# Fused attention and mixture of experts on one core: seven routing turns in each pair of heads instead of five

## The chip, the cores and the metric

The kernel runs on one core of a Trainium2 chip. The metric is the device time of one execution in microseconds (us). The engines of a core work side by side, each on its own queue in order: PE (TensorE, matmuls), DVE (VectorE), ACT (ScalarE), POOL (GpSimd) and SP (SyncE, which issues DMAs here). An instruction waits at the head of its engine's queue until what it reads is there and what it writes is free.

## The reference

Causal attention with a decay bias over 8 batches of 8 heads, 576 positions and 64 columns, and then a mixture of 16 experts in 4 groups, one expert for each of the 4608 tokens:

```python
scores = scale * np.matmul(q, k.transpose(0, 1, 3, 2))
cum = np.cumsum(np.maximum(s, 0.0), axis=-1)
bias = -(cum[:, :, :, None] - cum[:, :, None, :])
scores = np.where(causal, -1000000000.0, scores + np.minimum(bias, 0.0))
attn = np.exp(scores - np.max(scores, axis=-1, keepdims=True))
attn = attn / (np.sum(attn, axis=-1, keepdims=True) + 1e-09)
x = np.matmul(attn, v)                  # turned to (4608, 512)
g_idx = np.argmax(x @ w_group, axis=1)  # one group for each token
e_idx = np.argmax(xg @ w_expert[g], axis=1)  # one expert in that group
ye = np.maximum(xg[mask_e] @ w1[g, e], 0.0) @ w2[g, e]
out[tok_idx] = combined[:, None] * ye   # weighted by both softmax values
```

## The kernel before

Attention works through 64 heads, one head in each step, two heads (a pair) in an even and an odd step. In a step PE runs three kinds of matmuls, taken in turn: A, the scores of a head four steps ahead for its row maxima (`pm`, line 220, six items A0 to A5); B, the transposed scores of this step's head for the exponentials (`ps`, lines 276 and 278); and C, the product of the probabilities of the head before with the values (`po`, line 316).

What the other engines do with these goes through small queues of Python closures: a letter in the order pops one. `a` is DVE's maximum (`mx`, line 228), which reads a `pm` buffer and so gives it back; there are two such buffers, and `keep("a", 1)` pops the older maximum before a third matmul is written. `b` is ACT's exponential, `e` POOL's causal mask, `v` ACT's copies of `po`, `T` and `t` the turned row maxima (`pmt`, then `th` and `tl`, lines 248 and 249), `Y`, `Z`, `W`, `K` the softmax division on DVE (line 344, 350, 355 and `xT`, line 363), `L` and `M` the split of `xT` (ACT, then POOL's `xTl`, line 380), `O` and `o` the turned rows of x, `S` and `G` the split of the next heads' inputs on ACT and POOL.

The order is written out by hand in two strings, one for even and one for odd steps. `R` in them is a turn of the router, `J` a turn only late in the kernel. `Router.batch` is a generator: each turn runs it to its next `yield`, and a `yield n` lets n turns pass unused. One batch of 8 heads (four pairs) gives 576 tokens to route, in this order: the logits (`lg`), the tail's logits and its rows (`pr`), the logits turned (`plt`, three copies on DVE), the group maxima (lines 813 to 821, `lmx`, `eq`, `fx`), the choice as ones (`oh`, `hot`), the counts (`pc`, then `off` and `pos`), the places (`us`, `pl`), `col`, `rows`, two products on POOL, the first listing (`pi`) with `df`, the weights (`w` to `cw`, lines 909 to 916), their parts (`c3`, POOL), three products (`val`, one on POOL and two on DVE), and the last listing (`pw`). From the first turn to the last that makes 26 turns with the unused ones.

A pair has five turns, four pairs 20. What is left of a batch runs in one go, without the unused turns, when the next but one is about to write its `xT`: `rt.read` in `high` loops

```python
        while self.queue and self.logged < b - 1:
            self.step(True)
```

and so ends one batch and starts the next. In the order of the instructions this stands once in each batch, in an odd step, from the third batch's heads on. DVE, ACT, POOL and PE all follow the written order in this stretch; in the last steps of attention (from step 62) only PE does, and a scheduler orders the other engines.

After attention the experts run one after the other: tokens gathered by index, two matmuls, rows scattered to the output.

Of the kernel before, what the change touches and what calls it, by code (L numbers as in the profile page):

```python
# [19 lines left out]
B, H, S, D = 8, 8, 576, 64  # L20
# [33 lines left out]
def attn_moe(ctx, tc, qk, v, s, wr, w1, w2, out, stop_at=None, dbg=None):  # L54
# [23 lines left out]
    st.listed, st.added = {}, {}  # L78

    attention(tc, qk, v, s, wr, xs, st)  # L80
    if dbg is not None:
        nc.sync.dma_start(dbg['x'], xs)
# [32 lines left out]
def attention(tc, qk, v, s, wr, xs, st):  # L115
# [3 lines left out]
    with ExitStack() as ctx:  # L119
# [405 lines left out]
        for t in VT:  # L525
# [8 lines left out]

        ORDERS = [o.split() for i, o in enumerate((
            "b S R B0 R v b a A0 B2 v C0 e G a R a B3 T C1 A3 B1 A2 C2 b e t C3 v G C4 B4 J b D v e a a A1 "
            "W e A4 C5 e C6 b a A5",
            "C0 B2 A4 B0 A2 S v e O C1 B1 B3 v X o A0 a Y L b J A3 a v a e b C2 b R K e M C3 G e b Q "
            "e C4 v A1 Z B4 a R A5 C5 b C6 t a a"))]
        FIRST = [o.split() for i, o in enumerate((  # L540
            "B4 b e A1 a R B0 b e B1 b C0 A0 a R J T t C1 v v D A2 a R W C2 B2 b e O o Q A3 a R B3 b e e A4 a "
# [6 lines left out]
        for step in range(-LEAD, NH + 5):  # L548
            m, a = step + LEAD, step - 1
# [1159 lines left out]
```

## Time and profile before

| | us |
|---|---|
| runs of the kernel | 876.05, 881.72, 1372.2 |
| their median | 881.72 |
| the profiled execution | 876.57 |
| its span, first to last instruction | 874.8 |
| PE busy in the span | 840.2 (96%) |
| DVE busy | 718.9 (82%) |
| ACT busy | 615.7 (70%) |
| POOL busy | 603.2 (69%) |

The span is 1.8 us shorter than the profiled execution's time. Busy time of PE is made of matmuls whose ends are modelled; where a wait matters, the starts of neighbouring matmuls say more than the idle figure behind a row. A row of the timeline gives the start and the time in us, the engine, the line, the operation, the tiles written and read, and in brackets the idle time before it and what ended it.

### The profile page before, as it was taken

The numbers are of one execution on the slowest core, as the hardware profiler recorded it, in microseconds if no ns is written. First come the engines' busy times: TensorE is split into PE (matmuls) and PEld (weight loads), VectorE is DVE, ScalarE is ACT, GpSimd is POOL, SyncE is SP. The second block draws the span as 40 slices with busy tenths as digits, with TensorE's granted clock in tenths as the row PEclk, the third lists the DMA queues.
The fourth block names the chain that finished last, engine by engine and source line by source line (L and its number), as shares of the span: only waits on it lengthen the run. The fifth ranks groups of instructions, "written<-read, shape, count | busy, mean of one in ns | idle before, by whom it ended". The sixth has DMA issues, their size and how long they took to land. (4 is left out here: it accounts for less than half of the span.)

```text
span 874.8 us, 17801 instructions
## 1 busy us (share of the span) xinstructions
PE 840.2 (96%) x5601; PEld 774.2 (89%) x5601; DVE 718.9 (82%) x1975; ACT 615.7 (70%) x1397; POOL 603.2 (69%) x746
## 2 busy tenths in 40 slices
PE   4999999999999999998799999999999999999997
PEld 2788888888888888886689999999999999999996
DVE  7567787787878788787468799999999999999972
ACT  5668777787868777776656656776677767777760
POOL 9767677676877768545657956776777777777660
PEclk9999999999999999999899999999999999999999
DMA  6999898897979898723546655555656565666620
GB/s 189 256 246 253 233 243 225 218 244 195 251 208 241 224 238 209 180 63 121 173 137 216 219 175 202 203 175 187 228 202 195 182 220 198 235 211 223 218 94 26
DMA packets 81877, 174.06 MB, mean 199 GB/s; under 512 B 9676, under 2 KB 45132, under 8 KB 73584
## 3 DMA queue, kind: packets, MB, share of 16 engines
q1 hardware_dynamic: 71664, 152.93, 59.6%
q0 software_dynamic: 7488, 18.89, 5.8%
q10 hardware_dynamic: 2624, 1.03, 0.5%
q8 instruction: 46, 0.75, 0.3%
q14 instruction: 55, 0.45, 0.2%
HBM read 108.97 MB, written 19.69 MB: 147 GB/s over the span
## 5 line engine op out<-in xcount | busy, mean ns | idle before, releaser
L1016 POOL TENSOR_TENSOR wl<-raw,wh 128x512 fp32r<-128x512 f32 x163 | 209.7, 1299 | 82.4 <-ACT wh L1013 58.6
L1013 ACT CAST wh<-raw 128x512 fp32r<-128x512 f32 x256 | 153.9, 616 | 1.8 <-issue 1.8
L228 DVE CUSTOM_DVE_ANT_0 mx<-pm,mask 128x192 bf16<-128x192 f32 (+4 forms) x320 | 127.2, 418 | 31.4 <-PE pm L220 28.7
L1133 PE MATMUL ph<-xh,wh 128*128 128x256 f32 (+13 forms) x512 | 140.3, 300 | 1.8 <-DVE hl L1140 1.8
L220 PE MATMUL pm<-WA 66*128 66x288 f32 (+4 forms) x384 | 123.8, 355 | 15.3 <-DMA WA<-ch 9.5
L276 PE MATMUL ps<-WA 68*128 68x320 f32 (+4 forms) x384 | 135.9, 358 | 2.0 <-DMA WA<-tl 1.9
L1133 PE MATMUL ph<-xl,wh 128*128 128x256 f32 (+13 forms) x512 | 137.8, 301 | 0.0
L316 PE MATMUL po<-pt,VT 128*128 128x256 f32 (+3 forms) x512 | 119.4, 352 | 1.3 <-issue 1.0
L1212 PE MATMUL py<-hh,wh 128*128 128x256 f32 (+13 forms) x448 | 112.9, 302 | 0.0
L1212 PE MATMUL py<-hl,wh 128*128 128x256 f32 (+13 forms) x448 | 112.4, 301 | 0.0
L1139 ACT ACTIVATE hh<-ph 128x256 fp32r<-128x256 f32 (+13 forms) x128 | 53.3, 418 | 83.8 <-PE ph L1133 82.9
L278 PE MATMUL ps<-WB 128*128 128x320 f32 (+4 forms) x384 | 110.7, 301 | 0.0
L1265 DVE STREAM_TRANSPOSE yr<-yT 32x384 f32<-32x384 f32 (+1 forms) x208 | 104.6, 503 | 4.5 <-ACT yT L1209 0.4
L316 PE MATMUL po<-pu,VT 128*128 128x320 f32 (+1 forms) x384 | 105.5, 383 | 1.3 <-POOL pu L295 1.3
L1103 DVE STREAM_TRANSPOSE xt<-xg 32x256 f32<-32x256 f32 (+1 forms) x208 | 102.4, 492 | 2.7
L316 PEld LDWEIGHTS po<-pt,VT 128*128 128x128 f32 x512 | 88.2, 192 | 13.9 <-issue 1.5
L1133 PEld LDWEIGHTS ph<-xh,wh 128*128 128x128 f32 x512 | 95.9, 190 | 2.1 <-DVE hl L1140 1.9
L1133 PEld LDWEIGHTS ph<-xl,wh 128*128 128x128 f32 x512 | 95.2, 190 | 0.2
L162 POOL TENSOR_TENSOR WB<-r,hl 64x576 fp32r<-64x576 f32 x62 | 88.0, 1420 | 6.1 <-DMA WB<-hl 1.8
L1133 PE MATMUL ph<-xh,wl 128*128 128x256 f32 (+13 forms) x512 | 92.0, 299 | 0.0
L220 PEld LDWEIGHTS pm<-WA 66*128 66x128 f32 (+1 forms) x384 | 69.2, 193 | 25.1 <-DVE mc L228 9.8
L380 POOL TENSOR_TENSOR xTl<-xT,xTh 128x512 fp32r<-128x512 f32 x30 | 38.2, 1272 | 76.0 <-ACT xTh L376 55.4
(249 smaller groups left out, 2007.3 us busy)
## 6 DMA issues: line engine op xcount, KB each, us to landing
raw<-in_w_dram SPq DMA_DIRECT2D x64, 1024.0 KB
r<-in_qk_dram SPq DMA_DIRECT2D x32, 576.0 KB
WA<-hl SPq DMA_DIRECT2D x60, 288.0 KB
WB<-hl SPq DMA_DIRECT2D x60, 288.0 KB
VT<-in_v_dram SPq DMA_DIRECT2D x32, 384.0 KB
WB<-hl SPq DMA_DIRECT2D x64, 144.0 KB
xs<-xr SPq DMA_DIRECT2D x15, 512.0 KB
WA<-cumd SPq DMA_DIRECT2D x56, 4.5 KB
```

Of the source, the lines that this page charges most:

```text
L162: (nc.vector if p < 1 else nc.gpsimd).tensor_tensor(out=hl[:, 2] if part else WB[p % NBB][0:64, KA, h], in0=r[hr, part], in1=hl[hr, part]. ...
L220: nc.tensor.matmul(ps[:rows, :cw], WA[i][0:66, QA, h, QO + q0:QO + q0 + rows], WA[i][0:66, KA, h, QO + c0:QO + c0 + cw], start=True, stop= ...
L228: nc.vector.tensor_tensor_reduce(out=tmp[:rows, :cw], in0=ps[:rows, :cw], in1=mk[:rows], scale=1.0, scalar=-3.0e38 if c0 == 0 else mo, op0 ...
L276: nc.tensor.matmul(ps[:rows, o:o + w], WA[i][0:68, KA, h, QO + k0:QO + k0 + rows], WA[i][0:68, QA, h, QO + q0:QO + q0 + w], start=True, st ...
L278: nc.tensor.matmul(ps[:rows, o:o + w], WB[p % NBB][:, KA, h, k0:k0 + rows], WB[p % NBB][:, QA, h, q0:q0 + w], start=False, stop=True)
L316: nc.tensor.matmul(po[0][:, qa - base:qb - base], VT[p % NVT].rearrange("p t a d -> p (t a d)")[:, (3 * t + 1 + h) * 64:][:, 0:P], x[:, c: ...
L1013: self.casts.append(nc.scalar.copy(h[:, j], raw[:, j]))
L1016: self.low = lows[self.u, i, j] = nc.gpsimd.tensor_tensor(out=l[:, j], in0=raw[:, j], in1=h[:, j].bitcast(F32), op=ALU.subtract)
L1103: V.transpose(dst[:, 0:n, :, j], src[:, 0:n, :, i])
L1133: self.product = nc.tensor.matmul(pss[f][:, :cap], w[f // 4][:, c, (f % 4) * P:(f % 4 + 1) * P], x[:, c, :cap], start=(c == 0 and w is sel ...
L1212: self.product = nc.tensor.matmul(pss[c][:, :cap], w[2 + f // 4][:, f % 4, c * P:(c + 1) * P], x[:, f, :cap], start=(f == 0 and w is self. ...
L1265: V.transpose(dst[:, 0:n, :, i], src[:, 0:n, :, j])
```

## The change

Each of the two strings gets one more `R`: in the even step behind A4, in the odd step behind the first `S`.

```diff
         ORDERS = [o.split() for i, o in enumerate((
             "b S R B0 R v b a A0 B2 v C0 e G a R a B3 T C1 A3 B1 A2 C2 b e t C3 v G C4 B4 J b D v e a a A1 "
-            "W e A4 C5 e C6 b a A5",
-            "C0 B2 A4 B0 A2 S v e O C1 B1 B3 v X o A0 a Y L b J A3 a v a e b C2 b R K e M C3 G e b Q "
+            "W e A4 R C5 e C6 b a A5",
+            "C0 B2 A4 B0 A2 S R v e O C1 B1 B3 v X o A0 a Y L b J A3 a v a e b C2 b R K e M C3 G e b Q "
             "e C4 v A1 Z B4 a R A5 C5 b C6 t a a"))]
```

A pair then has seven turns and a batch's four pairs 28. Which turn of a batch falls where changes for all of them; from the last batch on every engine has the order of before. On each engine the set of instructions is the same.

On DVE, before, in the pair of steps in which `col` and `rows` run (`mx` is a maximum, `mc` its accumulator read back): `col` stands before the reciprocal of the odd step, `rows` before that step's last maximum.

```order
L228 ISA mx_2_0_3455,mc_155<-pm_2_0_3450,mask 128x320
L228 ISA mc_155 128x1
L868 TENSOR_TENSOR col_3462<-hot,u_3322 128x320
L350 RECIPROCAL rc_3473<-st_3446 128x18
L228 ISA mx_0_0_3478,mc_155<-pm_0_0_3471,mask_150 64x64
L228 ISA mc_155 64x1
L873 TENSOR_TENSOR rows_3480<-cols,pl_3341 128x640
L228 ISA mx_4_288_3487,mc_155<-pm_4_288_3482,mask,mc_155 128x288
```

The two places that `col` and `rows` leave hold other turns now.

On DVE, now, the same two turns: the first stands between the transpose of line 355 and the 64-wide maximum of the even step, the second between the last maximum of the even step and the 448-wide one of the odd step.

```order
L355 STREAM_TRANSPOSE st_3083<-rc_3111 128x576
L868 TENSOR_TENSOR col_3218<-hot,u_3152 128x320
L228 ISA mx_0_0_3223,mc_156<-pm_0_0_3213,mask_150 64x64
L228 ISA mc_156 64x1
L363 TENSOR_TENSOR xT_3231<-vals_2828,st_3083 128x576
L228 ISA mx_3_0_3240,mc_156<-pm_3_0_3216,mask 128x448
L228 ISA mc_156 128x1
L228 ISA mx_4_288_3247,mc_156<-pm_4_288_3225,mask,mc_156 128x288
L228 ISA mc_156 128x1
L873 TENSOR_TENSOR rows_3252<-cols,pl_3171 128x640
L228 ISA mx_3_0_3274,mc_156<-pm_3_0_3242,mask 128x448
```

Both now stand in places that held no turn before. In the other pairs of a batch the even place takes the copies of `plt`, the weights and the last lists, and the odd place the group maxima and the start of `c3`.

On PE, before, in the odd step in which one batch ends and the next begins: the last listing and the logits stand in one piece between two of the step's own matmuls.

```order
L886 MATMUL pw_3028<-val_2717,rows_2696 128x192
L733 MATMUL lg_3036<-xTh_2262,wr_sb 40x512
L734 MATMUL lg_3036<-xTl_2263,wr_sb 20x512
...
L737 MATMUL lg_3036<-xTh_2262,wr_sb 40x512
L220 MATMUL pm_4_0_3053<-WA_107 128x288
L220 MATMUL pm_2_0_3061<-WA_107 128x320
L316 MATMUL po_1_3069<-pt_118,VT_116 128x320
```

The burst is gone now, and its parts stand as turns of their own.

On PE, now, in an even step: the turned logits, which stood behind the burst, come right after the step's two neighbouring row-maximum matmuls.

```order
L278 MATMUL ps_4_0_2990<-WB_115 64x64
L220 MATMUL pm_0_0_3002<-WA_107 64x64
L220 MATMUL pm_3_0_3005<-WA_107 128x448
L801 MATMUL plt_3007<-ident,lT 128x128 x4
L316 MATMUL po_1_2978<-pu_121,VT_117 128x320 x2
L220 MATMUL pm_4_288_3021<-WA_107 128x288
```

The logits stand in the odd step there too, alone behind its 64-row items, the last listing has a turn of its own in an even step, and two turns lie between the two.

## Rows read from the trace of the kernel before

**Rows 1.** Windows, a plain pair and a batch's four: stretch, its length, busy times.

```profile
73.60:84.52 10.92, 10.92 (x72) 9.76 (x70) 7.98 (x30) 9.15 (x24) 8.13 (x13) 1.00 0.94 268
219.25:230.50 11.25, 11.25 (x79) 10.04 (x78) 9.60 (x39) 9.14 (x24) 7.71 (x13) 1.00 0.97 272
230.50:241.88 11.38, 11.38 (x77) 10.01 (x75) 10.60 (x36) 9.33 (x25) 10.69 (x15) 1.00 0.88 233
241.88:256.20 14.32, 14.12 (x94) 11.81 (x93) 10.58 (x39) 10.25 (x27) 9.18 (x18) 1.00 0.79 216
256.20:268.12 11.92, 11.73 (x76) 10.30 (x74) 10.10 (x39) 9.33 (x26) 7.91 (x13) 1.00 0.77 199
```

The busy times are those of PE, its weight loads, DVE, ACT and POOL, each with its instructions, then the granted clock, the DMA share and GB/s.

**Rows 2.** Timeline of PE in the burst between two batches.

```profile
201.42 0.59 PE L886 MATMUL pw<-val,rows 128*128 128x192 bf16 x5
...
203.69 0.45 PE L220 MATMUL pm<-WA 66*128 66x288 f32 x2
...
205.52 0.62 PE L787 MATMUL pr<-xtl,wr_f 128*20 128x64 f32 x8 [0.20 <-ACT xr L415]
...
206.27 0.38 PE L220 MATMUL pm<-WA 66*128 66x288 f32 x1
...
207.80 0.60 PE L801 MATMUL plt<-ident,lT 128*128 128x128 f32 x4
208.16 0.38 PE L220 MATMUL pm<-WA 66*128 66x288 f32 x1
```

**Rows 3.** Timeline of DVE in the plain pair.

```profile
78.07 0.08 DVE L228 DVE_READ_ACCUMULATOR2_ANT mc<- 64x1 f32 x1
...
79.83 0.08 DVE L228 DVE_READ_ACCUMULATOR2_ANT mc<- 128x1 f32 x1
80.39 0.62 DVE L228 CUSTOM_DVE_ANT_0 mx<-pm,mask 128x448 bf16<-128x448 f32 x1 [0.47 <-PE pm L220]
80.94 0.08 DVE L228 DVE_READ_ACCUMULATOR2_ANT mc<- 128x1 f32 x1
```

**Rows 4.** Timeline of PE in the plain pair, row-maximum matmuls.

```profile
76.34 0.25 PE L220 MATMUL pm<-WA 66*128 66x192 f32 x1
...
77.57 0.51 PE L220 MATMUL pm<-WA 66*64 66x64 f32 x2
...
78.75 0.53 PE L220 MATMUL pm<-WA 66*128 66x288 f32 x1
...
81.98 0.46 PE L220 MATMUL pm<-WA 66*128 66x288 f32 x2
```

**Rows 5.** Timeline of PE, the same two matmuls in the pair after the burst.

```profile
210.51 0.25 PE L220 MATMUL pm<-WA 66*128 66x192 f32 x1
...
212.06 0.75 PE L220 MATMUL pm<-WA 66*64 66x64 f32 x2 [0.15 <-DVE mc L228]
```

**Rows 6.** Timeline of DVE, a maximum's end and routing turns.

```profile
211.94 0.07 DVE L228 DVE_READ_ACCUMULATOR2_ANT mc<- 128x1 f32 x1
...
229.98 2.09 DVE L873 TENSOR_TENSOR rows<-cols,pl 128x640 bf16<-128x640 f32 x1
...
241.71 0.25 DVE L909 TENSOR_REDUCE w<-df 128x25 f32<-128x100 f32 x1
...
243.07 0.45 DVE L228 CUSTOM_DVE_ANT_0 mx<-pm,mask 128x288 bf16<-128x288 f32 x1
```

**Rows 7.** Timeline of POOL, in the plain pair and beside `rows`.

```profile
81.98 1.27 POOL L380 TENSOR_TENSOR xTl<-xT,xTh 128x512 fp32r<-128x512 f32 x1 [2.60 <-ACT xTh L376]
...
229.98 1.41 POOL L162 TENSOR_TENSOR hl<-r,hl 128x576 fp32r<-128x576 f32 x1
```

**Rows 8.** Instructions by tile, `eq` and `rows`: ns least, median, most.

```profile
L817 DVE TENSOR_TENSOR eq<-logit,lmx x8: 264/981/983, 109.4 to 433.7; 128x100 f32<-128x100 f32 x8
L873 DVE TENSOR_TENSOR rows<-cols,pl x8: 811/1578/2102, 122.2 to 442.3; 128x640 bf16<-128x640 f32 x8
```

**Rows 9.** Timeline of PE, the turned logits of the seventh batch.

```profile
400.57 0.66 PE L801 MATMUL plt<-ident,lT 128*128 128x128 f32 x4 [0.92 <-ACT lT L791]
```

## What the change should do to the time

> **What bounds the kernel now.** I read the windows by pair of heads first. TensorE (PE) fills its span in nearly every stretch: a pair of heads without routing takes 10.92 us and PE is busy for all of it, while VectorE (DVE) is busy for 7.98 us. The four pairs that carry one batch's routing take 11.25, 11.38, 14.32 and 11.92 us, 48.87 together, which is 5.19 us over four plain pairs [rows 1]. So a batch's routing costs 5.19 us in all, and nothing that the order does can give back more than the part of it in which PE waits.
>
> That part comes out of PE's timeline in the third and fourth pair, where the burst stands [rows 2]. The last listing matmuls and the next batch's logits run without a gap, 201.42 to 203.69, 2.27 us; the tail's logits and transposes take 0.75 us (205.52 to 206.27), the transposes back 0.36 us (207.80 to 208.16). With 0.33 us for the counts (the first pair's excess) and about 0.3 us for the first listing (an estimate: 5/8 of the work of the last, most of the second pair's 0.46 us), PE's own routing work is 4.0 us. What waits is 5.19 - 4.0 = 1.2 us a batch, some 7 us in the six batches that the change rearranges. That is 0.8% of the profiled execution: **the change cannot make the kernel 2% faster.**
>
> The Trainium skill (Perfetto Trace Analysis, Tensor Engine Instruction) says that a matmul's end in the trace is an estimate from its size. The trace agrees: the matmul at 212.06 shows 0.15 us idle before it, but it starts 1.55 us after its forerunner, against 1.23 us in a plain pair [rows 4, 5], so it waited 0.32 us. By the idle figures the waits of a batch would be about 0.4 us, 2 us in all; by the starts they are 7.
>
> **Where PE waits for DVE.** Each row-maximum matmul writes one of two pm buffers; DVE's maximum (mx) gives it back. The slack is read from a plain pair. After the 64-wide maximum DVE lets go at 78.15 (78.07 + 0.08) [rows 3], and the matmul that reuses that buffer starts at 78.75 [rows 4]: 0.60 us. The 448-wide maximum of the odd step lets go at 81.02, and its successor starts at 81.98: 0.96 us; before it DVE has 0.47 us idle (79.91 to 80.39). From a release to the matmul go 0.05 us, read where PE did wait: released at 212.01 (211.94 + 0.07) [rows 6], started at 212.06 [rows 5]. So lateness beyond 0.55 us at the 64-wide maximum, or beyond 0.47 + 0.9 at the 448-wide one, is paid by PE in full. At the other places of a pair DVE waits for PE and has more room; the five turns of before stand there.
>
> **The change part by part.** It adds a turn in the even step, on DVE between the transpose L355 and the 64-wide maximum, and one in the odd step, just before the 448-wide maximum. These are the two tightest places. No instruction is added or dropped; SP's and POOL's queues get the same DMAs and operations, a batch's rows of x go out a step or two sooner, and nobody reads them before the experts. A batch needs 26 turns and has 28 instead of 20, so no remainder is left to be run at once.
>
> *Removed:* the burst, with its waits: 7 us by the above. The tail's logits no longer stand behind a turned block that ACT has just to copy out, and the group maxima no longer stand ahead of th and tl. PE's 4.0 us a batch are only moved.
>
> *Added at the even place*, by the order of DVE:
> - plt: DVE, in order, waits there for PE's four transposes, which stand right after the two matmuls of the even step that follow each other. With the 0.36 us on PE and three small copies (0.4 us, an estimate at half of L817's best price each, [rows 8]) the 64-wide maximum comes some 0.8 us late against PE: 0.3 us of wait.
> - col: half as many elements as rows, so 0.4 us at its best price [rows 8], and DVE up to 0.3 us late already, since the turn before th stays there: 0.2 us.
> - the weights (L909 to L916), 241.71 to 243.07, 1.36 us [rows 6]: 1.36 - 0.55 = 0.8 us. Before, they lay where DVE had room.
> - the last lists: as plt, 0.2 us.
>
> *Added at the odd place:*
> - the group maxima (L813 to L821): their price hangs on L817, 0.26 us at best and 0.98 at the median [rows 8]. With three more of its size at 0.26 us each the turn takes 1.1 or 1.8 us.
> - rows: 0.81 us at best, 2.10 at worst [rows 8]. At 229.98 it starts together with a POOL operation of 1.41 us, and takes 2.09 [rows 6, 7]: it stands until POOL is through.
>
> Which end holds is read from POOL: at the odd place it is idle for 2.60 us until xTl at 81.98 [rows 7], so from 79.4 on, and the turn starts at about 79.9. I take the short ends, 1.1 and 0.81 us. Then the group maxima, with 0.55 us of lateness left from plt, come 0.55 + 1.1 - 0.47 = 1.2 us late against 0.9: 0.3 us, and 0.1 for the matmul behind. Rows: 0.5 + 0.8 - 0.5 = 0.8 against 0.9: 0.1 at most. For the later matmuls of these two odd steps, where DVE is still behind and 0.2 to 0.5 us of room is left, I add 0.3 us.
>
> Sum per batch: 0.3 + 0.2 + 0.8 + 0.2 + 0.4 + 0.1 + 0.3 = 2.3 us, six times: 13.8 us. Bounds: 1.0 (only the weights' wait is sure; a DVE that catches up sooner takes the rest) and 5 (below, both odd turns and the weights at their long price).
>
> The Trainium skill (SBUF — State Buffer, Who interferes with whom) states that a DVE instruction with two SBUF inputs and a GpSimd instruction that reads SBUF exclude each other for the whole instruction, whoever comes first. The two prices of rows fit that. By this rule the odd place, where POOL rests, has the short price, and my sum stands; if the long price belongs to the operation itself, the second rival holds.
>
> *The end of attention:* batch 6 is taken through sooner, with other work between its tail logits and its transposes, where PE now waits 0.92 us [rows 9]; I count 1.5 us less with the shorter waits around it, between 0 and 2.5. The last batch stands where it stood, and from there on the order is the same on every engine; PE is what the next stage waits for, so a shift arrives in full.
>
> Sum: 13.8 - 7 - 1.5 = **+5.3 us** on the profiled execution's 876.57 us: 881.9. The runs of before shown are 876.05 and 881.72 us (the third, 1372.2, is left aside) and the profiled one is at their low end; I put the median at 2 us over that sum: **884 us**, against 881.72 within measurement.
>
> **The rivals.**
> - *The burst's end pays.* DVE is in time at the new places (PE's own routing work, moved, gives it room), and PE waits 0.5 us a batch: 3 - 7 - 1.5 = -5.5 us, 871 us profiled, 873 as a median. For it: DVE is idle a quarter of a plain pair. Against it: that idle time does not lie at the new places.
> - *POOL is not idle there* (slower). The lock decides: if POOL's splits slide into the odd place (they follow ACT and DVE, which come later too), rows cost 2.1 us and the group maxima 1.8, and the weights' two products each stand behind a POOL operation at the even place. Per batch the waits are then about 1.5 (plt and maxima), 1.7 (col and rows), 1.7 (weights) and 0.2: 5.1 us, six times 31; 31 - 7 - 1.5 = +22 us, 899 profiled, 900 as a median. It passes 2% (17.5 us) from 4.3 us of wait a batch. For it: L817's median is the long price. Against it: the 2.60 us of POOL's idle time.
> - *The turns change nothing that PE feels*: waits as large as before, 876 to 879 us. That the turns stay empty is ruled out: the order moves the listings of every batch from the first to the sixth by several turns.
>
> **How the numbers follow.** My forecast 0.58, with 879 to 891; the burst's end 0.20; POOL not idle 0.12, of it two thirds past 2%; nothing felt 0.10. The range takes in the first rival's 873 and reaches into the second, to 896. Faster by over 2%, 0.01; within 2%, 0.91; slower by over 2%, 0.08. Two per cent is about what a measurement of this kernel can tell from no change.
>
> **What would show it.** Windows by pair over a batch: the pair of 14.32 us gone, the excess spread over all pairs, and in sum about 6.3 us a batch (4.0 + 2.3) in place of 5.19. PE's pm waits for DVE behind the weights (about 0.8 us by starts) and behind the group maxima. L817 at 0.3 and rows at 0.8 us. If they stay at 0.98 and 2.1, the second rival holds; if the sum over a batch is under 4.6, the first. The prediction is wrong if PE waits for ACT or POOL instead, which I count at nothing because both have idle time in every pair (ACT 9.15 and POOL 8.13 us busy of 10.92, [rows 1]).

## The result, and the profile after

The changed kernel takes 889.61 us (median of four runs, 884.56 to 892.48), the kernel before 880.04 us beside it (median of four; one of them, 1372.2 us, was disturbed and is left out of the ratio, and the median of the other three is 878.35). The ratio is **1.0135, 95% interval 1.0105 to 1.0164**: slower, by less than 2%. The profiled execution took 884.56 us, its span is 882.8 us; before it was 876.57 and 874.8.

Attention explains it. A step is counted from item B0 of its head, the 256 columns of transposed scores. From step 11 to step 60 the kernel before takes 297.32 us and the changed one 310.68: +13.4. From step 60 on they are alike to 0.8 us. Up to the start of step 5 it took 53.75 us after and 58.37 before. Two kernels with the order of before in this stretch take 58.4 and 55.2 us, six with the changed order 53.8 to 56.9, so these 4.6 us between the two profiled executions are put down to chance: 13.4 - 4.6 - 0.8 = 8.0. Without them the two differ by 12.6 us, near the 11.9 us of the ratio.

A batch is eight steps. In steady state it took 48.9 us before and takes 51.2 now. First the two steps of the plain pair of before, then the windows of the changed kernel by step, steps 28 to 35 (columns as in [rows 1]):

```profile
73.60:80.18 6.58, 6.58 (x40) 5.83 (x39) 4.42 (x16) 4.98 (x12) 5.59 (x9) 1.00 0.96 271
80.18:84.52 4.34, 4.34 (x33) 3.93 (x31) 3.56 (x14) 4.18 (x12) 2.54 (x4) 1.00 0.93 263
```

```profile
195.10:203.43 8.33, 8.29 (x55) 6.82 (x53) 4.78 (x20) 5.73 (x15) 4.73 (x7) 1.00 0.79 196
203.43:207.96 4.53, 4.53 (x32) 4.03 (x31) 4.43 (x16) 4.45 (x12) 3.04 (x4) 1.00 0.81 196
207.96:215.39 7.43, 7.41 (x48) 6.13 (x47) 7.15 (x32) 4.68 (x13) 4.70 (x9) 1.00 0.78 204
215.39:219.72 4.33, 4.33 (x32) 3.92 (x31) 4.09 (x17) 4.25 (x12) 2.70 (x4) 1.00 0.66 176
219.72:228.47 8.75, 7.81 (x46) 6.10 (x44) 7.23 (x24) 5.32 (x14) 7.53 (x15) 1.00 0.99 274
228.47:232.82 4.35, 4.35 (x32) 3.94 (x31) 3.65 (x16) 4.26 (x12) 2.85 (x5) 1.00 0.83 191
232.82:240.23 7.41, 7.30 (x46) 6.09 (x44) 6.31 (x20) 5.07 (x13) 6.44 (x9) 1.00 0.78 202
240.23:246.35 6.12, 6.12 (x40) 4.79 (x39) 3.55 (x16) 4.41 (x13) 3.55 (x6) 1.00 1.01 291
```

The four pairs are 12.86, 11.76, 13.10 and 13.53 us, where the same steps took 14.32, 11.92, 11.25 and 11.38 [rows 1]: the long pair is gone, and the last two pairs are 1.9 and 2.2 us longer. The batch's excess is 51.25 - 4 x 10.92 = 7.6 us where 5.19 stood. PE's own work for the routing is still 4.0 by the forecast's count, so PE now waits 3.6 us a batch (1.2 before, 2.3 forecast). By steps, as the excess over the plain step less PE's own routing work in it: tail logits and `plt` 0.6, group maxima 0.2, counts and `col` 0.5, `rows` 0, **the weights 1.9** (8.75 - 6.58 - 0.27), the next step 0, last lists 0.45, logits 0. Over half stands in one step.

What PE waits for there, in its timeline beside [rows 4]: from the 64-wide row-maximum matmul to its successor 2.49 us, against 1.18 in the plain pair.

```profile
224.34 0.51 PE L220 MATMUL pm<-WA 66*64 66x64 f32 x2
...
226.83 0.40 PE L220 MATMUL pm<-WA 66*128 66x288 f32 x1 [0.90 <-DVE mc L228]
```

And what DVE, ACT and POOL did in that step, in order of time; this answers to [rows 6]:

```profile
220.14 1.42 POOL L162 TENSOR_TENSOR hl<-r,hl 128x576 fp32r<-128x576 f32 x1
220.90 0.78 DVE L900 TENSOR_TENSOR df<-logit,lmx 128x100 f32<-128x100 f32 x1
221.71 0.29 ACT L904 ACTIVATE df<-df 128x100 f32<-128x100 f32 x1 [1.61 <-DVE df L900]
...
224.31 0.22 DVE L909 TENSOR_REDUCE w<-df 128x25 f32<-128x100 f32 x1
224.56 0.18 DVE L910 TENSOR_SCALAR w<-w 128x25 f32<-128x25 f32 x1
224.65 1.40 POOL L162 TENSOR_TENSOR WB<-r,hl 64x576 fp32r<-64x576 f32 x1
224.78 0.32 DVE L911 RECIPROCAL w<-w 128x25 f32<-128x25 f32 x1
225.13 0.96 DVE L913 TENSOR_TENSOR ws<-w,oh 128x20 f32<-128x20 f32 x1
226.12 0.17 DVE L915 TENSOR_REDUCE cw<-ws 128x5 f32<-128x20 f32 x1
226.33 0.22 DVE L916 TENSOR_TENSOR cw<-cw,w 128x5 f32<-128x5 f32 x1
226.47 0.21 DVE L228 CUSTOM_DVE_ANT_0 mx<-pm,mask 64x64 bf16<-64x64 f32 x1
```

The turn takes 224.31 to 226.47, 2.16 us, where 1.36 was forecast. The difference is one product of 20 columns, L913: POOL's split subtraction runs from 224.65 to 226.05, the product starts inside it at 225.13 and ends just after it, 0.96 us in place of 0.18. Only then come the 64-wide maximum and its read-back at 226.70, and with the latter PE's buffer. `df` stood behind POOL's first split in the same way (220.14 + 1.42 = 221.56; it ends at 221.68, 0.78 us in place of 0.26); that is 0.5 of the 1.61 us that ACT waited for it, and most of the rest is DVE's own wait of 1.07 us for the first listing.

The step of the counts and `col` lost its 0.5 us to a split too, and not to `col`. `oh` (L824), at a place of before, now begins with one:

```profile
206.68 1.41 POOL L162 TENSOR_TENSOR hl<-r,hl 128x576 fp32r<-128x576 f32 x1
206.75 1.46 DVE L824 TENSOR_TENSOR oh<-fx,desc 128x100 f32<-128x100 f32 x1
```

Its median over the batches is 1.46 us, 0.26 before. PE's counts wait 0.2 us for `hot`, which follows it, and DVE enters the step late. At `col` itself PE waits for nothing: from the 64-wide matmul to its successor it takes 1.18 us (212.59 to 213.77), as in the plain pair.

By tiles, for all batches, answering to [rows 8] (ns least, median, most):

```profile
L817 DVE TENSOR_TENSOR eq<-logit,lmx x8: 261/262/851, 101.2 to 441.5; 128x100 f32<-128x100 f32 x8
L873 DVE TENSOR_TENSOR rows<-cols,pl x8: 812/820/826, 112.9 to 450.3; 128x640 bf16<-128x640 f32 x8
L913 DVE TENSOR_TENSOR ws<-w,oh x8: 178/961/986, 122.6 to 458.0; 128x20 f32<-128x20 f32 x8
```

The group maxima and `rows` went from the long price to the short one, as forecast for the odd place; the weights went the other way. POOL does rest at the odd place, as in [rows 7]:

```profile
204.92 1.28 POOL L380 TENSOR_TENSOR xTl<-xT,xTh 128x512 fp32r<-128x512 f32 x1 [2.30 <-ACT xTh L376]
```

The view of waits, PE between 80 and 400 us, has one line (total, times, longest):

```profile
PE pm L220 <- DVE mc L228: 4.6, 5, 0.9
```

By its idle figures PE waits for DVE alone; ACT and POOL matter through DVE.

The end of attention, beside [rows 9], in PE's timeline:

```profile
407.26 0.65 PE L409 MATMUL px<-ident,xT 128*128 128x128 f32 x4 [0.82 <-DVE xT L363]
413.30 0.45 PE L886 MATMUL pi<-val,rows 128*128 128x128 bf16 x5 [0.53 <-DVE val L879]
420.64 0.57 PE L886 MATMUL pw<-val,rows 128*128 128x192 bf16 x5 [2.13 <-POOL val L930]
...
431.94 0.65 PE L409 MATMUL px<-ident,xT 128*128 128x128 f32 x4 [1.89 <-ACT xr L415]
```

The wait for `plt` (0.92 us) is gone, and the lists now wait 0.53 and 2.13 us for their products. Steps 60 to 62 take 19.87 us (19.82 before): nothing gained there. From the start of step 60 to the first matmul of the experts it is 38.5 us in place of 39.2.

### The profile page after: what moved, and what is told of

It is laid out like the page before. It is cut to its first block, busy times and chain, and to the rows that moved or that the text cites. A ratio compares the mean times of both kernels' runs of the same rounds, so it can differ in the third digit from the quotient of the medians.

```text
span 882.8 us, 17809 instructions
## 1 busy us (share of the span) xinstructions
PE 847.3 (96%) x5601; PEld 770.2 (87%) x5601; DVE 718.5 (81%) x1975; ACT 615.8 (70%) x1397; POOL 603.5 (68%) x746
## 5 line engine op out<-in xcount | busy, mean ns | idle before, releaser
L295 POOL TENSOR_SCALAR_AFFINE_SELECT pt<-pt 128x128 f32<-128x128 f32 (+2 forms) x192 | 69.3, 373 | 52.1 <-ACT pt L286 50.0
```

## The experiments

In all of them a batch is measured between the starts of steps 28 and 52, three batches, in the profiled execution; the ratio is to the kernel before, on the same chip. The two kernels without the split have one run each and no ratio.

| kernel | median us | ratio, 95% interval | batch us |
|---|---|---|---|
| before | 880.04 | | 48.9 |
| changed | 889.61 | 1.0135, 1.0105 to 1.0164 | 51.2 |
| weights at the odd place | 893.2 | 1.0176, 1.0145 to 1.0206 | 51.5 |
| seven turns, other places | 915.82 | 1.0432, 1.0400 to 1.0465 | 55.8 |
| five turns, fewer unused | 907.97 | 1.0362, 1.0337 to 1.0387 | 53.9 |
| split behind the turn | 897.32 | 1.0251, 1.0209 to 1.0293 | 52.15 |
| changed, no split | 885.42, one run | | 49.8 |
| before, no split | 874.1, one run | | 48.2 |
| exponential a turn later | 889.88 | 1.0147, 1.0120 to 1.0174 | 51.2 |
| the same, weights odd | 887.39 | 1.0118, 1.0092 to 1.0143 | 50.6 |
| weights cut in two | 889.3 | 1.0157, 1.0107 to 1.0208 | 51.0 |
| even turn alone | 895.65 | 1.0206, 1.0158 to 1.0253 | 54.1 |
| odd turn alone | 892.89 | 1.0190, 1.0149 to 1.0231 | 52.6 |
| cut, POOL's part at once | 889.41 | 1.0127, 1.0105 to 1.0149 | 50.1 |

The theory that I began with: the cost is lateness of DVE at the two tight places, most of it that of the weights in the even place, made longer by POOL's split. A first rival: any turn costs the same wherever it stands. A second: the turns wait for each other's results, and seven instead of five bring them too close together.

**The weights at the odd place.** One more unused turn behind the exponential:

```diff
         nc.scalar.activation(ex, df, AF.Exp)
-        yield 1
+        yield 2
```

> Seven turns as changed, but one more unused turn behind the exponential of the weights, so that the weights' turn falls on the odd place (POOL idle, 0.47 us of DVE idle time plus 0.9 us of room) instead of the even one. Theory (PE waits for DVE at the tight places, and the weights' turn there, 2.2 us long because one of its products stands behind a POOL split, makes 1.9 of the 3.6 us of waits in a batch): a batch of four pairs 49.4 us (49.1 to 49.8) instead of 51.25, the kernel within 0.3% of the one before. Rival (seven turns cost by their number and spread, whatever the place): a batch stays at 51.0 to 51.5 us and the kernel at 1.2 to 1.5% over the one before.

No gain: 51.5 us a batch. The even step is shorter (7.9 us in place of 8.75), and the odd step behind it longer by 1.5 (the next two steps change by -0.8 and +0.4, since every later turn moved too). Timeline of DVE and POOL there:

```profile
229.50 1.41 POOL L162 TENSOR_TENSOR WB<-r,hl 64x576 fp32r<-64x576 f32 x1
229.79 1.73 DVE L363 TENSOR_TENSOR xT<-vals,st 128x576 f32<-128x576 f32 x1
...
233.59 1.28 POOL L380 TENSOR_TENSOR xTl<-xT,xTh 128x512 fp32r<-128x512 f32 x1 [1.62 <-ACT xTh L376]
233.69 1.20 DVE L916 TENSOR_TENSOR cw<-cw,w 128x5 f32<-128x5 f32 x1
```

With the weights away, `xT` (0.76 us alone) runs into the split and takes 1.73, and at the odd place the last product, of five columns, meets POOL's `xTl`, for which POOL had rested. The rest at the odd place ends where the next turn begins. That slack alone prices the weights is refuted: at the place with more of it they cost as much.

**Seven turns at other places.** The two added turns next to turns of before, where DVE waits for PE (against the kernel before):

```diff
-            "b S R B0 R v b ... W e A4 C5 e C6 b a A5",
+            "b S R B0 R R v b ... W e A4 C5 e C6 b a A5",
-            "C0 B2 A4 B0 A2 S R v e O ... a R A5 C5 b C6 t a a"
+            "C0 B2 A4 B0 A2 S v e O ... a R R A5 C5 b C6 t a a"
```

> Seven turns in each pair, but the two new ones next to turns of before, at places where DVE has room (even: a second turn behind the one after B0; odd: a second one before A5). Theory: no burst and no tight place, so a batch takes 43.66 + 4.0 + 0.2 to 1.0 us = 47.9 to 48.7 us, against 48.88 before and 51.25 after; the kernel 0.0 to 0.7% under the one before. Rival (the number and spread of turns cost): 50.5 to 51.5 us a batch, 1% or more over the one before.

The expectation fell. The view of waits of this kernel, PE between 80 and 400 us:

```profile
PE pm L220 <- DVE mc L228: 20.5, 23, 1.6
```

Two turns in a row make one long turn, and a place that holds one in time doesn't hold two: 20.5 us where the changed kernel shows 4.6. The length is not all of it: L817 takes 1.02 us here, L865 1.41, `rows` 1.65 and L916 1.04, each behind a split in every batch measured (0.26, 0.17, 0.82 and 0.17 alone), and two of the three batches hold a fall of TensorE's clock (57.2 and 56.2 us, the one without 53.95). This kernel does not tell these parts from each other. Of the two ways to place seven turns, the change's is by far the better.

**Five turns, a batch in 20.** The order of before, with one unused turn less at each of five places (two are shown) and the first of the last three products in the turn of the parts; four unused turns stay:

```diff
         nc.scalar.copy(lT[:40], lg[:40])
-        yield 1
+        yield
 ...
-        yield 2
+        yield 1
         listed(0, 2, "pi")
 ...
         for j in range(3):
-            yield
+            if j:
+                yield
```

> The order of before with five turns, but six unused turns taken out of the batch's generator (and the first product in the turn of the parts), so that a batch fits into its 20 turns and no remainder is run in one go; every turn stands at a place of before. Theory (the burst's waits were 1.2 us a batch and the roomy places cost nothing): a batch 47.9 to 48.5 us, the kernel 0.3 to 0.7% under the one before. Rival (turns that follow each other sooner wait for each other): 48.9 us or more a batch, the kernel at or over the one before.

Here the second rival held: PE waits for POOL's products in each batch. PE's timeline, and the windows around it:

```profile
230.26 0.44 PE L886 MATMUL pi<-val,rows 128*128 128x128 bf16 x5 [1.84 <-POOL val L879]
```

```profile
228.00:230.00 2.00, 0.42 (x2) 0.12 (x2) 1.20 (x5) 0.41 (x1) 2.00 (x4) 1.00 1.03 314
...
231.00:232.00 1.00, 1.00 (x9) 1.00 (x8) 1.00 (x3) 0.00 (x0) 0.85 (x1) 0.81 1.06 265
232.00:234.00 2.00, 2.00 (x7) 1.61 (x7) 1.81 (x7) 1.93 (x5) 0.99 (x2) 0.50 0.89 280
...
236.00:238.00 2.00, 2.00 (x14) 1.81 (x13) 1.47 (x5) 0.97 (x3) 0.00 (x0) 1.00 0.58 127
```

PE does almost nothing for 2 us, and between 1 and 2 us after it has work again the granted clock falls to 0.50, the lower of its two levels (1.2 GHz), for some 3 us. The unused turn behind POOL's products is not waste: it gives POOL time. The 1.84 us are a third of the 5.0 us by which a batch is longer; the rest, waits for DVE and the falls of the clock among it, was not taken apart. In the changed kernel the unused turns stand where they stood, and PE's idle rows show no wait for POOL between 80 and 400 us, so this rival explains nothing of its 2.3 us.

**The split behind the new turn.** POOL's second split of a pair is written behind the even step's new turn instead of ahead of it:

```diff
-            ... C3 v G C4 B4 J ... A4 R C5 e C6 b a A5",
+            ... C3 v C4 B4 J ... A4 R C5 e G C6 b a A5",
```

> Seven turns as changed, but POOL's second split of the even step is written behind the new turn instead of ahead of it. Theory (the weights' product at the even place is locked out by that split): the product of line 913 falls from 0.96 to under 0.3 us, the weights' turn from 2.16 to about 1.4 us, and PE's wait behind it by about 0.8 us a batch; the split then slides into the odd place, so the group maxima and rows there should rise (rows from 0.82 to 1.3 or more), which may take the gain back: a batch 50.3 to 51.6 us. Rival (the product is long by itself): it stays at 0.96 us wherever POOL's split stands, and rows stay at 0.82.

Slower by 1 us a batch. L913 is free of the split in all steady batches, but the next product is not; timeline of DVE and POOL:

```profile
231.26 0.18 DVE L913 TENSOR_TENSOR ws<-w,oh 128x20 f32<-128x20 f32 x1
231.33 1.41 POOL L162 TENSOR_TENSOR WB<-r,hl 64x576 fp32r<-64x576 f32 x1
...
231.68 1.07 DVE L916 TENSOR_TENSOR cw<-cw,w 128x5 f32<-128x5 f32 x1
```

The weights' step is 8.77 us, as in the changed kernel, and the step of `col` is 1 us longer: `col` now takes 1.41 us (median) where it took 0.44. Order on paper does not keep the two apart; the engines' times do.

**No split at all.** In both kernels POOL writes zeros in place of the split's low part, from the second pair on (the low part of that operand is left out of the computation):

```diff
+                if p >= 1:
+                    nc.gpsimd.memset(..., 0.0)
+                    return
```

> The changed kernel, with POOL's subtraction that makes the low part of the inputs' split replaced by a fill with zeros from the second pair on (POOL then writes and does not read there); the low part is left out of the scores. Theory (DVE's operations with two SBUF inputs stand behind POOL operations that read SBUF; what costs most is the weights' turn, held up by the split): line 913 falls from 0.96 to about 0.2 us, the weights' turn to about 1.4, PE's wait behind it from 1.3 to about 0.8 us; a batch of four pairs 49.6 to 50.5 instead of 51.25. Rival (the operation is long by itself, or PE waits for something else): line 913 and the batch stay.

> The kernel before, with the same fill in place of POOL's subtraction (the low part is left out of the scores). Theory: rows falls from 2.10 to about 0.8 us and line 817 from 0.98 to 0.26 us, and the 0.56 us by which PE waits behind the group maxima are gone: a batch 48.2 to 48.5 instead of 48.88. So seven turns still cost 1.3 us or more a batch over five where the lock is mostly out of it. Rival (all of the change's cost is the lock): both kernels have the same batch, within 0.3 us.

Both came as expected. Windows of a batch: before with splits and without, then changed with splits and without; last the steps of the counts and of the weights in the changed kernel without splits:

```profile
193.00:241.88 48.88, 48.49 (x319) 42.16 (x317) 40.86 (x150) 38.05 (x98) 35.48 (x56) 1.00 0.85 230
193.29:241.46 48.17, 47.97 (x318) 42.00 (x317) 38.26 (x150) 38.11 (x97) 23.56 (x55) 1.00 0.93 232
```

```profile
195.10:246.35 51.25, 50.15 (x318) 41.82 (x317) 41.19 (x149) 38.17 (x97) 35.55 (x56) 1.00 0.84 221
199.02:248.78 49.76, 49.28 (x319) 41.70 (x317) 37.95 (x149) 38.11 (x97) 25.00 (x56) 1.00 0.88 225
211.88:218.80 6.92, 6.92 (x48) 6.08 (x47) 6.02 (x27) 4.57 (x12) 2.55 (x6) 1.00 0.83 220
223.13:231.11 7.98, 7.54 (x45) 6.03 (x44) 6.14 (x24) 5.49 (x14) 5.29 (x15) 1.00 0.99 268
```

Without splits the change costs 49.76 - 48.17 = 1.6 us a batch, with them 2.3 to 2.4. So 0.7 to 0.8 us a batch, a third of the change's cost, is the splits' doing: their removal is worth 1.4 to 1.5 us a batch after and 0.7 before. DVE does not stand behind them much longer than it did: its busy time falls by 3.2 us a batch in the changed kernel (41.19 to 37.95) and by 2.6 in the one before (40.86 to 38.26). What changed is which instructions meet them, and how little slack lies behind these. The step of the counts loses its wait (6.92 - 6.58 - 0.33 = 0.0), with `oh` at 0.26 us. The weights' step now waits 7.98 - 6.58 - 0.27 = 1.1 us, of it 0.8 at the 64-wide maximum (1.99 us from its matmul to the successor, for 1.18): there the forecast of 0.8, which had assumed POOL out of the way, holds.

**The exponential a turn later.** The unused turn moves from behind the exponential to ahead of it, so that ACT finds `df` ready; in a second kernel one more turn puts the weights at the odd place:

```diff
         ex = df
+        yield
         nc.scalar.activation(ex, df, AF.Exp)
-        yield 1
+        yield
```

> Seven turns as changed, but the weights' exponential has a turn of its own behind the differences, in place of the unused turn behind it, so that ACT has not to wait for DVE's differences (1.6 us, the copies of po and the exponentials queue behind it); the weights' turn stays on the even place. Theory: without that wait POOL's split in the even step ends before the weights' turn starts (in the plain pair it ends 4.6 us after the step begins, now 6.3), so line 913 takes 0.2 instead of 0.96 us; PE's wait behind the weights falls from 1.3 to about 0.8 us, and the even step's other losses (0.3 to 0.5 us) mostly go: a batch 49.8 to 50.4, the kernel 0.7% (0.4 to 1.0) faster than the changed one, about 0.6% over the one before. Rival (the split is late for another reason, or the wait is DVE's alone): line 913 stays at 0.96 and a batch at 51.

> As the kernel with the later exponential, and one unused turn behind it, so that the weights' turn falls on the odd place. Theory: with ACT on time xT is not locked out by the split any more (0.76 instead of 1.73 us), the weights' turn takes 1.4 us there against 0.47 us idle and 0.9 of room, if POOL's xTl does not come in between: a batch 49.0 to 49.8, the kernel within 0.5% of the one before. Rival (xTl starts before the last product, as it did when only the weights were moved): line 916 at 1.2 us and a batch at 50.3 or more.

The first went as the changed kernel did (51.2), though the product of L913 took its 0.18 us in every batch. Timeline of POOL and DVE:

```profile
226.39 1.40 POOL L162 TENSOR_TENSOR WB<-r,hl 64x576 fp32r<-64x576 f32 x1
226.79 1.03 DVE L911 TENSOR_SCALAR w<-w 128x25 f32<-128x25 f32 x1
```

The split begins earlier against the turn, and the addition of 1e-9 stands behind it in L913's place (0.18 us alone; line numbers are one higher here). The second is a little better, 50.6 us a batch, with the addition and both products short, but `xT` takes 1.4 to 1.9 us behind the split. What ACT waits for is therefore not the cause; it only shifts which of DVE's instructions meets the split.

**The weights cut in two.** The sum, the addition and the reciprocal in the even place, the products in the next odd one:

```diff
             V.reciprocal(wf, wf)
+        yield
+        with after(tc, st.routed):
             ws = T("ws", [NB, 4])
 ...
-        yield 2
+        yield
         listed(2, 5, "pw")
```

> The changed kernel, with the weights' turn cut in two: the sum, the addition and the reciprocal stay in the even step's new place (0.22 + 0.18 + 0.32 us, no operand pair that met POOL there), and the product with oh, its sum and the last product go to the next odd step's new place; one unused turn ahead of the last lists is dropped, so that every later turn but the three products stays where it was. Theory (the length of the turn against the 0.55 us of slack, and the stand behind POOL's subtraction, 0.78 us): of the 1.9 us of waits in the weights' step about 1.3 to 1.6 go, so a batch takes 49.7 to 50.0 us in place of 51.25 and the time is 881 to 884 us; xT, then earlier, may stand behind the same subtraction, and if it takes 1.3 us or more in place of 0.76 the gain is only 0.6 to 1.0 us (batch 50.3 to 50.7, 885 to 887 us). Rival (a turn in that place costs the same whatever its length, since it breaks DVE's row of maxima): a batch stays at 51.0 to 51.6 us, 888 to 892 us.

The weights' step fell by 0.9 us, to 7.85, with `xT` at 1.39 us behind the split, as the expectation allowed; but a batch fell by 0.2 only, since the step of the last lists is 0.7 us longer. PE's timeline:

```profile
237.00 0.57 PE L886 MATMUL pw<-val,rows 128*128 128x192 bf16 x5 [0.92 <-POOL val L932]
```

The dropped unused turn was POOL's time for the last products: the mechanism of the dropped turns again, in one place.

**One of the two turns alone.** Six turns a pair:

```diff
-            "W e A4 R C5 e C6 b a A5",
+            "W e A4 C5 e C6 b a A5",
```

(for the odd turn alone; for the even one the first string keeps its `R` and the second loses the one behind `S`)

> Only the even step's new turn, the odd step as before: six turns a pair, 24 a batch, two turns left for the run at a batch's end. Rows, weights and oh fall on the even place (slack 0.55 us). Theory: weights cost 0.7 to 1.9 us there (1.25 us alone, 2.16 us if a product stands behind POOL), rows 0.3 if short (0.82 us) and 1.5 if long (2.10 us), oh 0 to 0.9; of the 1.2 us of waits in the run at the batch's end about half stays: a batch of 50 to 51.5 us, 882 to 891 us. Rival (the odd place carries the cost of the change): 48.9 us or less, 876 to 880 us.

> Only the odd step's new turn, the even step as before: rows, weights, the last lists and oh fall on the odd place (slack 0.47 us ahead of the maximum and some 0.9 us behind it). Theory: rows 0 to 0.1 us if short, weights 0 to 0.8, lists 0.1, oh 0.1, half of the waits at the batch's end stays: 49.0 to 50.0 us a batch, 877 to 883 us. Rival (the even place and the odd place cost the same, by the turns that they hold): 50 to 51.5 us, as with the even turn alone.

Both expectations were too low: 54.1 and 52.6 us a batch, each more than both turns together. With 24 turns for 26, the tail's logits stand in the odd step as before (7.70 us there in two of the three batches of both kernels, and in before), L817 is back at 0.8 to 1.0 us, L865 takes 1.41 in place of 0.17, and the weights still meet POOL: in the even place the addition takes 1.42 us in two batches, with PE waiting after it, and L913 0.92 in the other one; in the odd place L916 takes 1.22 behind `xTl` and `xT` 1.73 behind the split, as in the first experiment. PE's wait behind the weights with the even turn alone:

```profile
295.54 0.40 PE L220 MATMUL pm<-WA 66*128 66x288 f32 x1 [1.42 <-DVE mc L228]
```

Behind it the granted clock falls to 0.50 for about 3 us, in two of the three batches measured. So the costs of the two turns don't add up from each alone; only 28 turns empty the run at a batch's end.

**Cut in two, POOL's part in the same turn.** As the cut, but the three parts for POOL follow the second half at once, and the unused turn ahead of the last lists is back:

```diff
             V.reciprocal(wf, wf)
+        yield
+        with after(tc, st.routed):
             ws = T("ws", [NB, 4])
 ...
-        yield
         with after(tc, st.routed):
             c3 = T("c3", [3, NB], BF16)
```

> As the weights' turn cut in two, but POOL's three parts of the weights follow in the same turn as the second half, and the unused turn ahead of the last lists is back, so that each later turn stands where it stands in the changed kernel. Theory: the weights' step stays at 7.85 us as with the cut alone (8.75 in the changed kernel), the 0.7 us that PE waited for POOL's last product ahead of the last lists go again (8.1 to 7.4 us), and a batch takes 50.3 us in place of 51.25: six batches give 5 to 6 us, 883 to 886 us, so still slower than before by some 0.5 to 1%. Rival (what the cut takes from the even place is given back on the odd one, as with the products): a batch of 51.0 us or more, 888 to 891 us. If the clock of TensorE falls below 1.00 in a stretch, as in four of the runs so far and in none of the others, the time is 2 us or more longer.

The batch came as expected, 50.1 us with the weights' step at 7.85 and the lists' at 7.2; the time did not, 889.41 us. From step 11 to 60 the kernel takes 304.5 us, 6.2 less than the changed one, and after that it loses them. DVE in the weights' step first, then PE at the end of attention:

```profile
226.20 1.39 DVE L363 TENSOR_TENSOR xT<-vals,st 128x576 f32<-128x576 f32 x1
```

```profile
420.03 0.96 PE L886 MATMUL pw<-val,rows 128*128 128x192 bf16 x5 [4.51 <-POOL val L931]
```

The last lists of the seventh batch wait 4.51 us for POOL's product, against 2.13 in the changed kernel; from the start of step 62 to the first matmul of the experts it takes 28.9 us in place of 24.4, and the granted clock is below 1.00 in five windows of 10 us between 410 and 460, in one in the changed kernel. Part of this is the changed kernel's luck: its profiled execution is the fastest of its four, and from step 60 on it takes 485.6 us, the least of all fourteen kernels (486.2 to 492.3 in the others, this one the most). The longer wait is not: it is 2.13 or 2.14 us in four of the kernels with the changed order's seven turns, and 3.45 to 4.51 in the four in which the exponential or the products of the weights stand later. The start-up took 3.2 us more, by chance. Why the product is later there, where a scheduler orders DVE, ACT and POOL, was not tried.

## Why the prediction was right, and where it was not

Sign, class and range held: +1.35% measured, 884 us forecast in 873 to 896, 889.61 us measured. The sign was hardly forecast, though (884 against 881.72 was called within measurement), and the range took in the first rival too. That the profiled executions differ by 8.0 us, near the 5.3 forecast, is luck: without the start-up it is 12.6, over twice the forecast. The mechanism held: PE bounds, no instruction is added, the burst goes, and DVE's lateness takes its place, nearly all of it in the even steps. The sizes did not all hold; step by step:

- *Removed, 1.2 us of waits a batch:* the burst is gone, and its waits with it. How many there were, and how many came, both rest on the 4.0 us counted as PE's own work.
- *plt, 0.3:* 0.6 in that step, most of it behind the transposes: DVE's place was right, its lateness half of what came.
- *col, 0.2:* nothing at `col`; 0.5 in its step, where `oh` stands behind a split, for which the sum had no term. It is gone without splits.
- *The weights, 0.8:* **1.9, the term that failed.** The turn was priced as in before (1.36 us less 0.55 of slack). In the new place L913 stands behind POOL's split. Without splits the wait is 1.1; cut in two, with `xT` behind the split, 1.0. The second rival named this ("the weights' two products each stand behind a POOL operation", 1.7 us), with a chance of 0.12 for it and the odd place together. The trace shows that the two went separately: the odd place short, the even place long.
- *The last lists, 0.2:* 0.45. *Group maxima 0.4, rows 0.1, later matmuls 0.3:* 0.2, 0 and 0: both turns at the short price as forecast, and DVE not late into them.
- *Sum, 2.3 us a batch:* 3.6, inside the bounds of 1.0 and 5. Net +2.35 us a batch in place of 1.1; steps 11 to 60 +13.4 us.
- *End of attention, -1.5:* -0.7 from step 60 to the experts. The wait for the transposes is gone, and PE waits 0.5 and 2.1 us for the products of the lists, which no step of the forecast had looked at.
- *ACT and POOL counted at nothing:* right for what PE waits for between 80 and 400 us (at the end of attention it does wait for POOL, 2.13 us), and wrong in what sets DVE's times. POOL's idle time was read at the odd place only; for the even place no row of POOL was looked up, though its splits stand in each pair.

The first step that failed is thus the weights' price in the even place, the second `oh`, which had no price, and the third, of 0.8 us once, the end of attention. That POOL's splits make the turns late is shown by the kernels without them (a third of the change's cost). The remaining 1.6 us a batch is put down to the turns' own length against the slack; that is argued from the steps, and of it only the weights were tried: cutting them took 0.9 us off their step with the splits running (with POOL's part at once a batch gets back 1.1 of its 2.35 us), and without splits their wait at the 64-wide maximum came as forecast.

The Trainium skill (SBUF — State Buffer, Who interferes with whom) has the rule cited in the prediction, and also that `tensor_scalar`, which adds the constant here, can under conditions take the port that DVE and GpSimd share. The traces agree: with splits running, a product of 20 columns took 0.96 us in place of 0.18, and the addition of a constant to 25 columns 0.98 to 1.42.

## What to carry to other kernels

A turn is not a fixed cost: before pricing it, read what POOL does at the very place where DVE will run it. Where POOL is two thirds busy with operations of 1.4 us, moving one small instruction out of its way puts another into it (in four experiments), so look for a way to do without the long operation (here it was left out for the test only; no kernel that computes everything did so), or keep the tight place free of instructions that can meet it. And count an unused turn as time given to another engine: one dropped behind POOL's products came back as a wait of 1.84 us a batch for POOL, one dropped ahead of the last listing as 0.92.

## What was not expected of the hardware

The granted clock of TensorE stayed at 1.00 from 80 to 400 us in the changed kernel, but fell to 0.50 (1.2 GHz) for stretches of some 3 to 7 us in four others: with five turns and fewer unused behind five of six waits of 1.84 us, with seven turns at other places behind two neighbouring waits of 1.02 and 0.98 us or one of 1.58 (not behind each such), with the even turn alone behind one of 1.42 us, and with the odd turn alone once, behind 0.87 and 0.58 us. The kernel with the weights at the odd place has waits of up to 1.1 us in each batch and no such fall; the runs don't tell what separates them. A wait of PE can thus cost more than its length: with five turns the two batches with a fall took 54.2 and 54.3 us, the one without 53.3. Behind 400 us the clock falls in every kernel.

A DVE operation on two tiles in SBUF, or an addition of a constant, of 5 to 25 columns and 0.17 or 0.18 us alone, took 0.9 to 1.4 us where it began early in a POOL subtraction (in nine of the kernels), and ended within 0.05 us of POOL's end, as the rows of 225.13 and 226.79 show. Not every DVE instruction waits: the reciprocal of 224.78 began inside the same subtraction as L913 and took its usual 0.32 us, and with the split behind the turn the sum of L915 began inside one at 231.47 and took its usual 0.17.
